# Convolution stem, forward and backward, on one core: more split leaves in both gradients, the second gelu by channel halves, x sums of batch 1 made in its input gradient, and a new order

## The chip, the cores and the metric

The kernel runs on one core of a Trainium2 chip. Its engines are TensorE (PE; PEld is its weight load), VectorE (DVE), ScalarE (ACT), GpSimd (POOL) and SyncE (SP), which in this kernel only issues DMAs. The metric is the device time of one launch in microseconds.

## The reference

```python
# x: 2 x 16000 x 256, w: 31 x 256 x 256, grad_out: 2 x 7985 x 256, bf16
def _fwd_reference(x, w, gn_gamma, gn_beta):
    h = sum over i of einsum('blc,cd->bld', x[:, i:i + 2 * L:2, :], w[i])   # L = 7985
    mu = h summed over l / L;  var = (h - mu) ** 2 summed over l / L
    h = (h - mu) / sqrt(var + 1e-5) * gn_gamma + gn_beta
    return gelu(h, approximate=True)
out, vjp = jax.vjp(_fwd_reference, x, w, gn_gamma, gn_beta)
return out, *vjp(grad_out)        # out, dx, dw, dgamma, dbeta
```

(The loop over the 31 taps is written here as one sum.) So there are three large products: the strided convolution itself, its gradient for x, and its gradient for w. Between the first and the other two lies the gelu with its normalization over the 7985 positions, forward and backward.

## The kernel before

Each of the three large products is made with fewer multiplications by splitting: taps and positions are grouped, and out of products of sums and differences the wanted ones are put together again. There are three **branches**, named A, B_ and C_, and inside a branch three **leaves** of the same names. Where a leaf is itself split once more ("split leaves" below), PE has fewer or shorter matmuls, and DVE and ACT have more sums and copies.

**Stages.** The forward product runs first, batch 0 and then batch 1, 0 to 408 us. Batch 0's gelu and its backward are done beside batch 1's forward product. Then come the input gradient (G0 for batch 0, G1 for batch 1, 408 to 801) and the weight gradient (W, 801 to the end). Batch 1's gelu (`gelu_short`) has no forward product beside it: it runs in G0, DVE lines 920 and 923 and ACT lines 916, 926 and 943. It ends with sums over all positions (`elem_finalize`, line 978 on); only when these are there can batch 1's gradient planes be made (`e_comp`, lines 1015 and 1017), spread (line 1033), subtracted (`g_sums`, line 1082) and multiplied in G1.

**Input gradient.** A batch has four chunks c, each with two halves pr and three branches. For a unit (c, pr, br), PE writes into PSUM tiles (line 1136). In a unit that the set `GOC` names ("both"), one product `pt` is shared: ACT copies its half (`g_delta`, line 1165), DVE subtracts it from the other tile (`g_seed`, line 1199), and at the end ACT keeps the results in `HO` (line 585), onto which DVE adds `GSB` (line 1213). In another unit the seed is a copy by ACT (line 585, from PSUM to PSUM), and the evacuation is an addition of 1024 on DVE (line 1217). Before, `GOC` names all of batch 1, chunk 3 of batch 0, and the branch B_ of its chunks 0 to 2.

**Leaves for W.** What W needs as stationary operands are the leaves of the gradient, transposed. `dl_turn` makes them, nine per chunk, 72 in all: two DMA transposes on SP's queue (line 319) fill one of the buffers `DNO`, and two stores of 128 KB on POOL's queue (line 314) bring it to DRAM (`dld`). W loads them from there.

**Weight gradient.** Nine nodes n, each with leaves; the set `NODES` says which leaves are split. x tiles are loaded from DRAM (1 MB each) and added on DVE (`w_add`, line 1316), or loaded as sums (`xsd`, `xssd`) that `x_sums` (line 754) has made in the forward stage, for batch 0 alone. `pair_x` (lines 1417, 1421), `pair_d` (1437), `leaf_d` (1520, 1525), `w_pairs` (1453) and `w_both` (1461) are the sums and copies around W's matmuls (line 1351).

**Order.** The program is first collected as a list of operations, each with the operations that it depends on. A table of numbers, `SEQUENCE`, then says in which order they are emitted, and that order is pinned on every engine. So what each queue does next is written in this table, and not decided anew. Nearly all DMAs, large loads and stores among them, are issued by SP in that order, and SP waits in order: behind an issue that waits for a semaphore, all later ones stand.

## Time and profile before

| what | value |
|---|---|
| runs | 1115.04, 1113.68, 1113.3 us; median 1113.68 us |
| span of the profiled execution | 1111.2 us |
| PE busy | 1086.2 us (98%) |
| DVE busy | 919.9 us (83%) |
| ACT busy | 578.9 us (52%) |
| granted TensorE clock | 1.00 throughout |
| DMA moved | 256.16 MB, mean 231 GB/s |

The profiled execution has only its span; the runs' median is 2.5 us more. An engine's share over the whole span is a mean over the stages, and the prediction goes through them one by one. In a row of a group, the number behind x is the count, then come the busy time, the mean ns of one instruction, the idle time ahead of it and what ended that.

### The profile page before, as it was taken

Reading aid. Unit: us, or ns where it says so; the run is one execution under the profiler, and the core shown is the slowest. Engines: PE = TensorE matmul, PEld = TensorE weight load, DVE = VectorE, ACT = ScalarE, POOL = GpSimd, SP = SyncE. Lnnn points to the kernel's source line nnn. Section 1 sums busy time; section 2 is a strip of 40 time slices with the busy share of each in tenths; the row PEclk is TensorE's granted clock in tenths of the full one; section 3 lists DMA queues with packets and bytes.
Section 4 is the critical chain, followed back from the end, with each engine's and each line's share of the span. In section 5 each row is a group of like instructions: output and inputs, shape, how many; then the busy total and the mean of one; then the engine's idle time right before and its main releaser. Section 6 shows DMA issues by size and latency. Waiting matters only on the chain.

```text
span 1111.2 us, 18967 instructions
## 1 busy us (share of the span) xinstructions
PE 1086.2 (98%) x7623; PEld 749.8 (67%) x7672; DVE 919.9 (83%) x900; ACT 578.9 (52%) x880; POOL 129.3 (12%) x233
## 2 busy tenths in 40 slices
...
GB/s 231 198 188 249 233 275 267 219 167 162 209 166 219 240 328 270 274 252 265 217 225 237 179 203 183 157 201 197 278 293 137 270 156 298 303 254 279 282 253 207
DMA packets 348806, 256.16 MB, mean 231 GB/s; under 512 B 234327, under 2 KB 315869, under 8 KB 343517
## 3 DMA queue, kind: packets, MB, share of 16 engines
...
HBM read 114.62 MB, written 84.45 MB: 179 GB/s over the span
## 4 chain that ended last, share of the span: by engine, by line
PE 89%; DVE 5%; issue 2%; DMA 1%; SPq 1%; ACT 1%; DVEq 0%
PE ps L1136 34%; PE ps L506 34%; PE ps L1351 21%; SPq L314 1%; DMA out_dram<-arena 1%; DVE arena L1437 1%; DVE ps L1461 1%; DMA arena<-in_w_dram 1%; DVE arena L1421 1%; DVE arena L1380 1%; DVE arena L1525 0%; DVE arena L581 0%; DVE arena L1417 0%; DVE arena L448 0%; DVE arena L1316 0%
## 5 line engine op out<-in xcount | busy, mean ns | idle before, releaser
L506 PE MATMUL ps<-arena 128*128 128x256 bf16 (+4 forms) x3464 | 396.6, 278 | 11.2 <-DMA arena<-in_x_dram 4.7
L1136 PE MATMUL ps<-arena 128*128 128x512 bf16 (+1 forms) x1787 | 388.1, 376 | 5.7 <-ACT ps L1165 3.6
L506 PEld LDWEIGHTS <-arena 128*128 128x128 bf16 x3464 | 338.2, 98 | 69.4 <-DMA arena<-in_x_dram 5.8
L1136 PEld LDWEIGHTS <-arena 128*128 128x128 bf16 x1824 | 178.5, 98 | 215.1 <-issue 2.9
L1351 PE MATMUL ps<-arena 128*128 128x256 bf16 (+1 forms) x2372 | 301.6, 289 | 3.4 <-DVE arena L1520 1.8
L1351 PEld LDWEIGHTS <-arena 128*128 128x128 bf16 x2384 | 233.2, 98 | 71.9 <-issue 2.3
L585 ACT ACTIVATE arena<-ps 128x1024 bf16<-128x1024 f32 (+1 forms) x121 | 122.1, 1022 | 213.0 <-PE ps L1351 77.3
L464 DVE TENSOR_TENSOR arena<-arena 128x2064 bf16<-128x2064 bf16 (+7 forms) x131 | 162.7, 1265 | 24.2 <-PE ps L506 23.0
L314 POOL DMA_DIRECT2D dld<-arena x144 | 104.6, 728 | 246.7 <-DMA arena<-arena 229.4
L1199 DVE TENSOR_TENSOR ps<-ps,arena 128x1024 f32<-128x1024 f32 x36 | 44.3, 1232 | 64.2 <-PE ps L1136 53.2
L1082 DVE TENSOR_TENSOR arena<-arena 128x1032 bf16<-128x1032 bf16 (+1 forms) x114 | 89.5, 813 | 9.5 <-POOL arena L1049 4.3
L551 ACT ACTIVATE ps<-ps 128x256 f32<-128x256 f32 x89 | 36.7, 412 | 85.6 <-PE ps L506 84.5
L1316 DVE TENSOR_TENSOR arena<-arena 128x4096 bf16<-128x4096 bf16 x30 | 68.3, 2287 | 0.5 <-DMA arena<-in_x_dram 0.3
L1165 ACT COPY ps<-ps 128x512 f32<-128x512 f32 x84 | 48.1, 575 | 33.7 <-PE ps L1136 30.0
L323 POOL MEMSET arena<- 128x104 bf16 (+11 forms) x52 | 12.0, 249 | 414.8 <-DVE arena L464 157.6
L923 DVE TENSOR_TENSOR arena<-arena 128x2048 bf16<-128x2048 bf16 (+1 forms) x48 | 57.5, 1197 | 3.0 <-ACT arena L926 1.3
L605 ACT ACTIVATE arena<-ps 128x512 bf16<-128x512 f32 (+1 forms) x64 | 37.0, 582 | 32.7 <-PE ps L506 28.2
L885 DVE TENSOR_TENSOR arena<-arena 128x2048 bf16<-128x2048 bf16 (+1 forms) x40 | 47.7, 1197 | 4.0 <-ACT arena L879 1.7
L1437 DVE TENSOR_TENSOR arena<-arena 128x2048 bf16<-128x2048 bf16 x40 | 48.5, 1220 | 2.4 <-PE ps L1351 2.4
L1461 DVE TENSOR_TENSOR ps<-ps,arena 128x1024 f32<-128x1024 f32 x24 | 29.1, 1227 | 19.5 <-PE ps L1351 19.5
L1453 ACT COPY ps<-ps 128x256 f32<-128x256 f32 x54 | 19.0, 360 | 47.8 <-PE ps L1351 46.7
L1525 DVE TENSOR_TENSOR arena<-arena 128x4608 bf16<-128x4608 bf16 x16 | 40.6, 2554 | 0.0
...
## 6 DMA issues: line engine op xcount, KB each, us to landing
...
dld<-arena POOLq DMA_DIRECT2D x144, 128.0 KB, 4.4
...
```

The source lines that it names most:

```text
L314: lambda: e.dma_start(out=out, in_=in_), dma=np_ * ns / 16e3 * 1.03, ns=ns, tp=SH[pk], slack=slack)
L464: lambda: nc.vector.tensor_tensor(out=o, in0=a, in1=b, op=ALU.add))
L506: yield nc.tensor.matmul(ps[:, dh, cs], lhsT=wt, rhs=mv, start=s0, stop=False, skip_group_check=True)
L585: lambda: nc.scalar.activation(out=out, in_=ps, func=ACT.Copy, scale=scale))
L885: add("DVE", dve(nf), [o], [a, b_], lambda: V.tensor_tensor(out=o, in0=a, in1=b_, op=op))
L923: add("DVE", dve(nf), [o], [a, b_], lambda: V.tensor_tensor(out=o, in0=a, in1=b_, op=op))
L1082: lambda: nc.vector.tensor_tensor(out=o, in0=a, in1=b, op=ALU.subtract))
L1136: yield nc.tensor.matmul(ps[:, e, 0:wide], lhsT=lt, rhs=mv, start=s0, stop=False, skip_group_check=True)
L1165: add("ACT", act(512), [o], [i], lambda: nc.scalar.copy(out=o, in_=i))
L1316: add("DVE", dve(4096), [o], [a, b], lambda: nc.vector.tensor_tensor(out=o, in0=a, in1=b, op=ALU.add))
L1351: yield nc.tensor.matmul(ps[:, s, c0:c1], lhsT=lt, rhs=mv, start=s0, stop=False, skip_group_check=True)
L1437: add("DVE", dve(2048), [o], [u, v], lambda o=o, u=u, v=v: nc.vector.tensor_tensor(out=o, in0=u, in1=v, op=ALU.subtract))
```

## The change

- `GOC` now names every unit, so that the twelve units of batch 0 with c below 3 and branch A or C_ become "both" units: 36 matmuls in place of 44, 24 evacuations of 1024 on DVE and 12 seeding copies on ACT less, and 12 shared products with 24 copies of 512 on ACT, 12 seeding subtractions, 24 keeps, 12 additions of 2048 and 6 subtractions of 2064 (`third_two`) more. The sums of w for the outer products (`w2_outer`) are all made when G begins.
- `NODES` has three more leaves, (4, C_), (5, C_) and (3, C_): each 96 matmuls of 256 columns in place of 64 of 512.
- `gelu_short` works on one half of the channels at a time: each of its loads, stores, DVE operations and its sigmoid becomes two of half the size. The tiles of its ring are half as large.
- `x_sums` is called for batch 1 too, eight times in G1, with a buffer of its own (`XB`). W loads these sums in place of raw x rows, and eight additions of 4096 fall away.
- To make room, the leaf buffers `DNO` go from four to two, and `GSD`, which had two, to one; several others move. In batch 0 `HO` is a single buffer in all chunks.
- `SEQUENCE` is new, 3585 operations where there were 3357.

The pieces of the new order that the prediction speaks of, as they stand in the program. First SP's queue in G0, near the end of batch 1's gelu. `DMA_TRANSPOSE arena<-arena 128x4x128` is one transpose of a leaf, `waits DMASW...` a wait for stores that POOL has issued, `dyd` and `hd` are the gelu's stores and loads. Before:

```order
L319 DMA_TRANSPOSE arena<-arena 128x4x128 [waits DMAHW0_49,DMASW5_49,DMASW3_49]
L319 DMA_TRANSPOSE arena<-arena 128x4x128 [waits DMAHW1_49]
L319 DMA_TRANSPOSE arena<-arena 128x4x128 [waits DMAHW2_49]
L314 DMA arena<-hd_2_66 128x2x1024 [waits DMAHW3_49,DVE_49,Activation_49]
L319 DMA_TRANSPOSE arena<-arena 128x4x128 [waits DMASW7_49,DMAHW4_49,DMASW6_49,DVE_49]
L319 DMA_TRANSPOSE arena<-arena 128x4x128 [waits DMAHW5_49,DMASW1_49,DMASW0_49]
L319 DMA_TRANSPOSE arena<-arena 128x4x128 [waits DMAHW6_49]
L314 DMA arena<-hd_2_66 128x2x1024 [waits DMAHW7_49,DVE_49,Activation_49]
L319 DMA_TRANSPOSE arena<-arena 128x4x128 [waits DMAHW0_49]
```

And after:

```order
L327 DMA_TRANSPOSE arena<-arena 128x4x128 [waits DMAHW2_49,DMAHW4_49,DMASW7_49,DMASW6_49]
L322 DMA dyd_1_73<-arena 128x1024 [waits DMAHW3_49]
L327 DMA_TRANSPOSE arena<-arena 128x4x128 [waits DMAHW5_49,DMASW1_49,DMASW0_49]
L327 DMA_TRANSPOSE arena<-arena 128x4x128
L327 DMA_TRANSPOSE arena<-arena 128x4x128 [waits DMAHW6_49]
L322 DMA out_dram<-arena 128x4096 [waits DMAHW7_49,DVE_49]
L322 DMA arena<-hd_2_66 128x1024 [waits DMAHW0_49,Activation_49]
L322 DMA arena<-dyd_3_71 128x2048 [waits DMAHW1_49,Pool_49]
L327 DMA_TRANSPOSE arena<-arena 128x4x128 [waits DMAHW2_49,DMASW3_49,DMASW2_49]
L327 DMA_TRANSPOSE arena<-arena 128x4x128 [waits DMAHW5_49,DMAHW3_49]
L327 DMA_TRANSPOSE arena<-arena 128x4x128 [waits DMAHW4_49,DMASW5_49,DMASW4_49]
```

The gelu's transfers now come in halves (128x1024 in place of 256x1x1024 and 128x2x1024). Where the waits for POOL's stores once spoke of stores that lay several leaves back, each leaf now waits for the two stores of the leaf before the last one.

Second, DVE at the end of batch 1's gelu; L978 and L991 are the reduction of its sums, L1082 and L1095 the subtractions of G, L1217 an evacuation of G0, L923 and L937 the gelu. Before:

```order
L1082 TENSOR_TENSOR arena<-arena 128x2x516
L1082 TENSOR_TENSOR arena<-arena 128x8x258 x2
L452 TENSOR_TENSOR arena<-arena 128x2048
L978 TENSOR_REDUCE small<-esum_113 128x4
L1082 TENSOR_TENSOR arena<-arena 128x2x516
L1217 TENSOR_TENSOR arena<-ps,arena 128x2x512
L980 TENSOR_TENSOR small<-stats,small 128x2
```

After (the first seed of batch 1 stands 25 rows behind the reduction there, and 54 rows behind it before):

```order
L1226 TENSOR_TENSOR arena<-arena 128x4x512
L937 TENSOR_TENSOR arena<-arena 128x4x232
L934 TENSOR_SCALAR arena<-arena 128x4x232
L937 TENSOR_TENSOR arena<-arena 128x4x232 x3
L991 TENSOR_REDUCE small<-esum_115 128x4
L993 TENSOR_TENSOR small<-stats,small 128x2
L994 TENSOR_TENSOR small<-small 128x2
L995 TENSOR_TENSOR small<-stats 128x2
L996 TENSOR_TENSOR small<-stats,small 128x2
```

The reduction moved behind the last operations of G0, and its small operations follow one on the other where G0's work lay between them.

Third, SP's queue at the passage from G1 to W; `dld` are the leaves that W loads, `in_x_dram` 128x4096 the x rows for `x_sums`, 128x8x512 a raw x tile for W. Before:

```order
L319 DMA_TRANSPOSE arena<-arena 128x4x128
L314 DMA arena<-dld_0_85 128x2304 [waits DMAHW6_49,PE_49]
L314 DMA arena<-dld_0_76 128x2560 [waits DMAHW7_49,PE_49]
L314 DMA arena<-dld_0_85 128x2560 [waits DMAHW0_49,PE_49]
L314 DMA out_dram<-arena 104x4096 [waits DMAHW1_49,DVE_49]
L314 DMA arena<-in_x_dram 128x8x512 [waits DMAHW5_49,DMAHW3_49,DMAHW2_49]
L319 DMA_TRANSPOSE arena<-arena 128x4x128 [waits DMASW4_49,DMASW3_49]
L314 DMA out_dram<-arena 128x4096 [waits DMAHW4_49]
L314 DMA arena<-in_x_dram 128x8x512 [waits PE_49]
```

After:

```order
L327 DMA_TRANSPOSE arena<-arena 128x4x128 [waits DMAHW1_49,DMAHW2_49,DMASW1_49,DMASW0_49]
L327 DMA_TRANSPOSE arena<-arena 128x4x128 [waits DMAHW3_49]
L322 DMA xssd_97<-arena 128x1024 [waits DVE_49]
L322 DMA dld_4_80<-zt_116 2x256 [waits DMAHW4_49]
L327 DMA_TRANSPOSE arena<-arena 128x4x128 [waits DMAHW5_49]
L322 DMA arena<-in_x_dram 128x8x512 [waits DMAHW6_49,PE_49]
L322 DMA arena<-in_x_dram 128x4096 [waits DMAHW7_49,DMAHW3_49]
L327 DMA_TRANSPOSE arena<-arena 128x4x128 [waits DMAHW0_49,DMAHW2_49,DMASW3_49,DMASW2_49]
L322 DMA arena<-dld_0_76 128x2304 [waits DMAHW1_49,PE_49]
L327 DMA_TRANSPOSE arena<-arena 128x4x128
L322 DMA arena<-dld_0_85 128x2304 [waits PE_49]
```

The last calls of `x_sums` with their loads and stores now stand between the last leaf transposes and the first leaves that W loads.

The diff, without the table and without lines that only carry addresses of other buffers along:

```diff
@@ -37,111 +37,119 @@
 SEQUENCE = """
...
@@ -348,19 +356,19 @@
-    HO = [sb(119232, 2, 4, 512), sb(GREG + 16704, 2, 4, 512)]
+    HO = [sb(119232, 2, 4, 512), sb(GREG + 20544, 2, 4, 512)]
     GSD = [sb(o, 512, dt=FP32) for o in (111040, 113088)]
-    DNO = {True: [sb(GREG + 28928 + 2048 * i, 2, 2, D) for i in range(4)], False: [sb(GREG + o, 2, 2, D) for o in (0, 2048, 25088, 27136)]}
+    DNO = {True: [sb(o, 2, 2, D) for o in (208960, 113088)], False: [sb(o, 2, 2, D) for o in (208960, 113088)]}
...
@@ -747,16 +755,19 @@
 
-    def x_sums(f):
-        load(XA, xblk(0)[:, f].rearrange("p (k r) c -> p k r c", k=2), 1 << 20, 4096)
-        for o, v in ((XA[:, :, 1:4:2], XA[:, :, 0:4:2]), (XA[:, :, 0], None)):
-            u = XA[:, :, 2] if v is None else v
+    XB = sb(GREG + 28736, 2, 4, 512)
+
+    def x_sums(f, b=0):
+        xa = (XA, XB)[b]
+        load(xa, xblk(b)[:, f].rearrange("p (k r) c -> p k r c", k=2), 1 << 20, 4096)
+        for o, v in ((xa[:, :, 1:4:2], xa[:, :, 0:4:2]), (xa[:, :, 0], None)):
+            u = xa[:, :, 2] if v is None else v
             add("DVE", dve(o.free_size()), [o], [o, u], lambda o=o, u=u: nc.vector.tensor_tensor(out=o, in0=o, in1=u, op=ALU.add))
-        load(xs_d[:, f, :, 0:2], XA[:, :, 0:2], 1 << 19, 2048)
-        load(xs_d[:, f, :, 2], XA[:, :, 3], 1 << 18, 1024)
-        o, u = XA[:, 0, 1:3], XA[:, 1, 1:3]
-        add("DVE", dve(1024), [o], [o, u], lambda: nc.vector.tensor_tensor(out=o, in0=o, in1=u, op=ALU.add))
-        load(xss_d[:, f], o, 1 << 18, 2048)
+        load(xs_d[b][:, f, :, 0:2], xa[:, :, 0:2], 1 << 19, 2048)
+        load(xs_d[b][:, f, :, 2], xa[:, :, 3], 1 << 18, 1024)
+        o, u = xa[:, 0, 1:3], xa[:, 1, 1:3]
+        add("DVE", dve(1024), [o], [o, u], lambda o=o, u=u: nc.vector.tensor_tensor(out=o, in0=o, in1=u, op=ALU.add))
+        load(xss_d[b][:, f], o, 1 << 18, 2048)
 
...
@@ -826,7 +837,7 @@
             return [sb(base - (n - j) * size, *shape) for j in range(n)]
-        tiles = [ring_of(k, 2, 4, HM) for k in rings]
+        tiles = [ring_of(k, *((2, 4, HM) if b == 0 else (4, HM))) for k in rings]
         gts = ring_of(ngt, 4, 2, XM)
...
@@ -848,8 +859,12 @@
                 oo = oos[n % len(oos)]
-                (gelu_unit if b == 0 else gelu_short)(b, c, e, [r[n % len(r)] for r in tiles],
-                                                      gt.rearrange("p k d f -> p d k f")[:, :, :, off:off + HM], oo)
+                go = gt.rearrange("p k d f -> p d k f")[:, :, :, off:off + HM]
+                if b == 0:
+                    gelu_unit(b, c, e, [r[n % len(r)] for r in tiles], go, oo)
+                else:
+                    for dh in range(2):
+                        gelu_short(b, c, e, dh, [r[(2 * n + dh) % len(r)] for r in tiles], go[:, dh])
                 n += 1
...
@@ -901,20 +916,19 @@
 
-    def gelu_short(b, c, e, tiles, go, oo):
+    def gelu_short(b, c, e, dh, tiles, go):
 
         full = tiles
-        h, y, s, z, go = (t[:, :, :, 0:wd] for t in (*tiles, go))
-        hv, dv = (d[b][c][:].rearrange("p (d e f) -> p d e f", d=2, e=2)[:, :, e] for d in (h_d, dy_d))
-        load(full[0].rearrange("p d k f -> p d (k f)"), hv, 524288, 2048, "ACT")
-        for dh in range(2):
-            for o, k, fn in ((y, 7, ACT.Identity), (z, 9, ACT.Square)):
-                sc, bi = st(b, k, dh), st(b, k + 1, dh)
-                add("ACT", act(4 * wd, 0.18), [o[:, dh]], [h[:, dh], sc, bi],
-                    lambda o=o, dh=dh, sc=sc, bi=bi, fn=fn: SC.activation(out=o[:, dh], in_=h[:, dh], func=fn, bias=bi, scale=sc))
-        nf = 8 * wd
+        h, y, s, z, go = (t[:, :, 0:wd] for t in (*tiles, go))
+        hv, dv = (d[b][c][:].rearrange("p (d e f) -> p d e f", d=2, e=2)[:, dh, e] for d in (h_d, dy_d))
+        load(full[0].rearrange("p k f -> p (k f)"), hv, 262144, 2048, "ACT")
+        for o, k, fn in ((y, 7, ACT.Identity), (z, 9, ACT.Square)):
+            sc, bi = st(b, k, dh), st(b, k + 1, dh)
+            add("ACT", act(4 * wd, 0.18), [o], [h, sc, bi],
+                lambda o=o, sc=sc, bi=bi, fn=fn: SC.activation(out=o, in_=h, func=fn, bias=bi, scale=sc))
+        nf = 4 * wd
 
...
@@ -933,14 +947,13 @@
         tt(s, y, go, ALU.mult)
-        load(dv, full[2].rearrange("p d k f -> p d (k f)"), 524288, 2048, "POOL")
+        load(dv, full[2].rearrange("p k f -> p (k f)"), 262144, 2048, "POOL")
         tt(y, s, h, ALU.mult)
         for i, t, jk in ((0, s, h), (1, y, y)):
-            for dh in range(2):
-                a0, v, j = esum[b][:, dh, i, u:u + 1], t[:, dh], jk[:, dh]
-                add("ACT", act(4 * wd, 0.19), [j, a0], [v],
-                    lambda j=j, v=v, a0=a0: SC.activation(out=j, in_=v, func=ACT.Copy, accum_out=a0))
+            a0 = esum[b][:, dh, i, u:u + 1]
+            add("ACT", act(nf, 0.19), [jk, a0], [t],
+                lambda jk=jk, t=t, a0=a0: SC.activation(out=jk, in_=t, func=ACT.Copy, accum_out=a0))
 
...
@@ -1060,7 +1073,7 @@
             for lf in (C_, A, B_):
-                ds = DNO[4 * b + c < 3]
+                ds = DNO[4 * b + c < 4]
                 o = ds[tbc[0] % len(ds)]
...
@@ -1183,17 +1196,17 @@
 
-    gsc = [0]
+    gsc, bnow = [0], [0]
 
     def g_delta(pt):
-        gsc[0] += 1
-        g_copy(GSD[gsc[0] % 2], pt[:, 0])
+        gsc[0] = 0
+        g_copy(GSD[gsc[0]], pt[:, 0])
 
             return
-        t = GSD[gsc[0] % 2]
+        t = GSD[gsc[0]]
         i = bass.AP(tensor=t.tensor, offset=t.offset, ap=[list(t.ap[0]), [0, 2], [1, 512]])
...
@@ -1203,7 +1216,7 @@
         both = (b, c, br) in GOC
-        ho = HO[pr if both else 0]
+        ho = HO[pr if b else 0]
         r2 = 0 if br == A else 1
...
@@ -1222,7 +1235,7 @@
     G3 = {(b, br, B_) for b in range(NB) for br in ORDER}
-    GOC = {(b, c, br) for b in range(NB) for c in range(NCK) for br in ORDER if 4 * b + c >= 3 or br == B_}
+    GOC = {(b, c, br) for b in range(NB) for c in range(NCK) for br in ORDER if (b, c, br) not in ()}
 
...
@@ -1304,7 +1318,7 @@
-    NODES = {(6, C_), (5, A), (0, A), (0, C_), (1, A), (2, A), (3, A), (4, A), (6, A), (7, A), (7, C_), (8, C_)}
+    NODES = {(6, C_), (5, A), (0, A), (0, C_), (1, A), (2, A), (3, A), (4, A), (6, A), (7, A), (7, C_), (8, C_), (4, C_), (5, C_), (3, C_)}
...
@@ -1329,8 +1343,8 @@
         else:
-            if b == 0 and B_ in (i1, i2):
-                load(t, xs_d[:, :, k3, {(C_, B_): 0, (B_, A): 2, (B_, C_): 1}[i1, i2]], 1 << 20, 1024)
+            if B_ in (i1, i2):
+                load(t, xs_d[b][:, :, k3, {(C_, B_): 0, (B_, A): 2, (B_, C_): 1}[i1, i2]], 1 << 20, 1024)
                 return t
...
@@ -1501,8 +1515,8 @@
             for b in range(NB):
-                if b == 0 and n in (6, 7):
-                    load(XSUM[b], xss_d[:, :, n - 6], 1 << 20, 1024)
+                if n in (6, 7):
+                    load(XSUM[b], xss_d[b][:, :, n - 6], 1 << 20, 1024)
                 else:
...
@@ -1626,13 +1640,12 @@
         load_w2(br)
-        if br == B_:
-            for lf in (C_, A):
-                w2_outer(lf, (B_,))
+        for lf in (C_, A):
+            w2_outer(lf, (MIR[br],))
     for i in range(2):
     e_load(0, 0)
-    ge = gelu_batch(1, GREG, *RINGS[1], *PACE[1])
+    ge = gelu_batch(1, GREG + 20544, *RINGS[1], *PACE[1])
     for b, c, pr, br, leaf in input_grad():
...
@@ -1650,9 +1663,8 @@
             dl_turn(b, c, leaf)
-        if (b, c, pr, br) == (0, 2, 1, A):
-            for lf in (C_, A):
-                w2_outer(lf, (A, C_))
+        if b == 1 and br == A:
+            x_sums(2 * c + pr, 1)
     plan.stage = "W"
```

19 lines of the change are left out of this document (10 added, 9 removed), and 218 rows, old and new, of the table SEQUENCE.

## The prediction

> **What bounds the kernel now.** I read the page's busy times and the engine shares of the chain that ended last, then the table of stretches, then groups of instructions, then what SP's queue waited for.
>
> ```profile
> span 1111.2 us, 18967 instructions
> PE 1086.2 (98%) x7623; PEld 749.8 (67%) x7672; DVE 919.9 (83%) x900; ACT 578.9 (52%) x880; POOL 129.3 (12%) x233
> ...
> PE 89%; DVE 5%; issue 2%; DMA 1%; SPq 1%; ACT 1%; DVEq 0%
> ```
>
> TensorE (PE) is busy for 1086.2 of 1111.2 us and makes 89% of the chain. So less PE work is worth its full length wherever the other engines can follow. Whether they can is read stage by stage (columns: stretch, its length, busy us and instructions of PE, PEld, DVE, ACT, POOL, the granted clock, DMA share, GB/s):
>
> ```profile
> 418.70:622.20 203.50, 201.84 (x935) 93.24 (x953) 180.81 (x210) 162.72 (x198) 65.41 (x110) 1.00 1.00 244
> 450.00:500.00 50.00, 49.08 (x229) 22.69 (x233) 46.63 (x50) 44.73 (x56) 17.53 (x28) 1.00 1.06 260
> 570.90:622.20 51.30, 51.04 (x237) 23.45 (x240) 39.49 (x58) 26.39 (x34) 17.33 (x27) 1.00 0.94 232
> 618.00:801.00 183.00, 182.10 (x840) 83.83 (x856) 101.39 (x107) 103.84 (x135) 55.59 (x95) 1.00 0.81 195
> 801.00:1111.20 310.20, 302.12 (x2376) 233.25 (x2385) 274.38 (x189) 73.11 (x107) 2.69 (x4) 1.00 0.83 249
> 1000.00:1050.00 50.00, 50.00 (x433) 42.27 (x432) 49.71 (x37) 11.27 (x19) 0.00 (x0) 1.00 0.86 276
> ```
>
> The first row is the input gradient of batch 0 (G0), from its first seeding subtraction on DVE (418.7) to the first of batch 1 (622.2). There PE is full, and DVE (89%), ACT (80%) and the DMA engines (1.00) nearly so. In batch 1's part (G1, 618 to 801) DVE and ACT are a little over half busy. The weight gradient (W, 801 on) has DVE at 88%, and around 1000 us PE and DVE are both full.
>
> **Part 1: less PE work, in G0 and in W.**
>
> ```profile
> L1136 PE MATMUL ps<-arena 128*128 128x512 bf16 (+1 forms) x1787 | 388.1, 376 | 5.7 <-ACT ps L1165 3.6
> L1136 PEld LDWEIGHTS <-arena 128*128 128x128 bf16 x1824 | 178.5, 98 | 215.1 <-issue 2.9
> L1351 PE MATMUL ps<-arena 128*128 128x256 bf16 (+1 forms) x2372 | 301.6, 289 | 3.4 <-DVE arena L1520 1.8
> L1351 PEld LDWEIGHTS <-arena 128*128 128x128 bf16 x2384 | 233.2, 98 | 71.9 <-issue 2.3
> ...
> L1351 PE MATMUL ps<-arena 128*128 128x512 bf16 x372 | 84.4, 379 | 0.6
> ...
> 519.61 10.53 PE ps L1136 x49
> ```
>
> The mean ns of one matmul overlaps its neighbours, so the price is busy time over number. Each matmul has its weight load, and 1824 loads stand against 1787 recorded matmuls: some records are missing, and the load count is the right divisor. The last row, a piece of the chain, gives 10.53/49 = 0.215 us per 512-column matmul. For W I take the 372 recorded 512-column ones at that price (80.0), which leaves 301.6 - 80.0 = 221.6 us for the other 2012, 0.110 each.
>
> Twelve units of G0 (three chunks, two branches, two halves) go from 44 to 36 matmuls, 84 of 512 columns and 12 of 256 in all: 84 x 0.215 + 12 x 0.110 = 19.4 us. Three more W leaves go from 64 matmuls of 512 columns to 96 of 256: 192 x 0.215 - 288 x 0.110 = 9.6 us. Together **-29.0 us** of PE work; weight loads stay 7672, and 98 ns of one still fits behind 110.
>
> The Trainium skill, "TensorE: Matmul & The Clock Gate", section "Back-to-back issue gap", gives sustained spacings of about 131 ns at 512 columns and 81 ns at 128. By these a 512-column matmul costs at most 50 ns more than a 256-column one, and the saving would be an estimated 276 x 0.05 = 13.8 us at most. The rows, 215 against 110 ns, do not agree with that at all, so this reading gets no chance of its own.
>
> **Part 2: what G0 pays.** The durations (mean ns of one stands after the comma):
>
> ```profile
> L1199 DVE TENSOR_TENSOR ps<-ps,arena 128x1024 f32<-128x1024 f32 x36 | 44.3, 1232 | 64.2 <-PE ps L1136 53.2 <-issue 8.9 <-ACT arena L1165 1.5
> L1082 DVE TENSOR_TENSOR arena<-arena 128x2064 bf16<-128x2064 bf16 x26 | 31.6, 1230 | 3.1 <-POOL arena L323 1.6 <-PE ps L1136 1.2
> L1217 DVE TENSOR_TENSOR arena<-ps,arena 128x1024 bf16<-128x1024 f32 x24 | 28.8, 1219 | 6.5 <-PE ps L1136 5.4 <-issue 1.0
> L1213 DVE TENSOR_TENSOR arena<-arena 128x2048 bf16<-128x2048 bf16 x20 | 24.4, 1222 | 19.2 <-ACT arena L585 19.1
> L923 DVE TENSOR_TENSOR arena<-arena 128x2048 bf16<-128x2048 bf16 x36 | 44.0, 1223 | 1.8 <-ACT arena L916 0.4 <-ACT arena L926 0.3
> L452 DVE TENSOR_TENSOR arena<-arena 128x1024 bf16<-128x1024 bf16 x20 | 13.4, 684 | 0.0
> L1165 ACT COPY arena<-ps 128x512 f32<-128x512 f32 x36 | 20.8, 587 | 8.6 <-PE ps L1136 8.3
> L1165 ACT COPY ps<-ps 128x512 f32<-128x512 f32 x84 | 48.1, 575 | 33.7 <-PE ps L1136 30.0 <-remote 2.6 <-DVE arena L1217 0.4
> L585 ACT ACTIVATE arena<-ps 128x1024 bf16<-128x1024 f32 x86 | 86.8, 1021 | 77.7 <-PE ps L1136 53.7 <-PE ps L506 14.8 <-remote 7.9
> L585 ACT ACTIVATE ps<-ps 128x1024 f32<-128x1024 f32 x18 | 18.1, 1006 | 5.3 <-PE ps L1136 3.3 <-remote 1.6 <-PE ps L506 0.4
> L926 ACT ACTIVATE arena<-arena 128x2048 bf16<-128x2048 bf16 x12 | 22.9, 1909 | 0.9 <-DVE arena L923 0.8
> L943 ACT ACTIVATE arena<-arena 128x1024 bf16<-128x1024 bf16 x24 | 25.1, 1047 | 2.1 <-DVE arena L923 2.0
> ```
>
> DVE gains 12 seeds (14.8), 6 subtractions of 2064 (7.4) and 12 additions of 2048 (14.7), and loses 24 evacuations of 1024 (-29.3): +7.6. A gelu operation of 2048 becomes two of half the width, 2 x 0.684 against 1.223, +0.145 each; 64 such operations, the shorter ones and the scalar ones taken at the same surplus, give +9.3. ACT gains 24 copies (12 x 0.587 + 12 x 0.575 = 13.9) and 24 keeps (24.5), loses 12 keeps inside PSUM (-12.1), and pays 16 split sigmoids (2 x 1.047 - 1.909 = 0.185 each, 3.0): +29.3. So ACT has about 192 us of work in a part that PE could now do in 184. From 162.7/203.5 = 80% ACT would have to go to 100%, and every keep and copy waits for a matmul.
>
> The order moves one thing more:
>
> ```profile
> 570.90 0.18 DVE L978 TENSOR_REDUCE small<-esum 128x4 f32<-128x32 f32 x1
> ...
> 622.20 1.23 DVE L1199 TENSOR_TENSOR ps<-ps,arena 128x1024 f32<-128x1024 f32 x1 [1.48 <-PE ps L1136]
> ```
>
> The reduction that ends batch 1's gelu sums stood 54 rows ahead of batch 1's first seed on DVE, with 39.5 us of DVE work between. It now stands 25 rows ahead, some 15 us by these durations. So less preparation of G1 lies in the part, and DVE's rows up to that seed, priced alike, come to 179 us where they were 176; but the chain of reduction, small operations, first products, sums and first matmuls of G1 has little other work left to hide behind. Bounds for the part: 184 (all of the 19.4 gained) and above 203.5 (nothing gained, and G1 starts late). The 50 us from 450 show the fullest that ACT has been over such a length, 44.73/50 = 89%; 192/0.97 = 198 is my value, nearer to the old length: 5.5 of the 19.4 are kept, a loss of **+13.9**.
>
> **Part 3: sums of x rows in G1.** Each of eight calls adds one load of 1 MB, 1 MB of stores, an addition of 2048 and two of 1024 on DVE: 8 x (1.22 + 2 x 0.684) = 20.7 us. DVE's 101 of 183 us hide that. The 16.8 MB are harder: W moved 249 GB/s at share 0.83, so 300 at full share, which makes 56 us of share, while G1 has 183 x 0.19 = 35 free. G0 shows that PE can stay full at share 1.00, so the bounds are 0 and 56 - 35 = 21. No reader waits for these sums in G1, so I take +4, nearer to nothing. At the passage to W two of these calls now share SP's queue with the first leaves that W loads: bounds 0 and one more set of transfers, some 7 us; I take +2.
>
> **Part 4: W.**
>
> ```profile
> L1316 DVE TENSOR_TENSOR arena<-arena 128x4096 bf16<-128x4096 bf16 x30 | 68.3, 2287 | 0.5 <-DMA arena<-in_x_dram 0.3
> L1437 DVE TENSOR_TENSOR arena<-arena 128x2048 bf16<-128x2048 bf16 x40 | 48.5, 1220 | 2.4 <-PE ps L1351 2.4
> L1461 DVE TENSOR_TENSOR ps<-ps,arena 128x1024 f32<-128x1024 f32 x24 | 29.1, 1227 | 19.5 <-PE ps L1351 19.5
> ```
>
> Eight additions of 4096 go (-18.3). The new split leaves add six of L1437 (7.3), two of 2048 and two of 4096 for the x pairs (2.4 + 4.6), and six of L1461 (7.4): +3.4. DVE then has 277.8 us in 300.6, 92%; the row from 1000 shows PE full beside a full DVE, so I let 1.1 of the 9.6 be lost (bounds 0 and 9.6).
>
> **Part 5: two transposed-leaf buffers instead of four.** A leaf (72 of them, all in G) is turned by two transposes on SP's queue, and stored by two DMAs on POOL's; only when these have landed is its buffer free.
>
> ```profile
> SPq L319 <- DMA dld<-arena: 41.3, 16, 7.2
> ...
> SPq L319 <- DMA dld<-arena: 36.9, 13, 7.2
> ...
> L319 SPq DMA_TRANSPOSE arena<-arena x177: 1188/1270/7553, 232.9 to 1096.4; - x177
> ...
> L314 POOL DMA_DIRECT2D dld<-arena x144: 723/723/943, 423.2 to 824.8; - x144
> ...
> dld<-arena POOLq DMA_DIRECT2D x144, 128.0 KB, 4.4
> ...
> DMA to landing us min/median/max: 2.2/4.4/8.3
> ...
> dld<-arena POOLq DMA_DIRECT2D x68, 128.0 KB, 4.7
> ```
>
> The first row is of the whole span, the second of 618 to 801: with four buffers SP already stood 36.9 us there for one to come free, and PE did not feel it. With two, pairs of leaves pass in 36 turns, and G lasts 393 us less what is gained: a turn T may take 391/36 = 10.9 us before the queue falls behind. T is the issue of a transpose (1.27), its landing (no row; taken as that of the store), the issue of a store (0.72) and its landing: 1.27 + 4.4 + 0.72 + 4.4 = 10.8 at the medians, 11.4 with the 4.7 of G1; 6.3 at the least and 18.6 at the most. Behind a waiting transpose stand, on SP's queue, the loads of dy and h, the out stores and now the x rows. I take 10.8, the medians over all: +0, with no room left.
>
> The Trainium skill, "DMA: Bandwidth & Descriptors", section "Anatomy of one DMA — SWDGE (gpsimd) path", puts such a store at about 2.0 us fixed and its bytes over 436 GB/s: an estimate of 2.3 for 128 KB. By it T would be 6.6 and the smaller ring could not slow anything. The trace agrees at its least value, 2.2, and not at its median of 4.4, which counts here.
>
> **The sum.** -29.0 + 13.9 + 4 + 2 + 1.1 + 0 = -8.0, a span of 1103.2. The runs' median, 1113.68, lies 2.5 above the profiled span, so **1106 us**.
>
> **The rivals.**
> *All of it shows.* ACT's and DVE's extra work goes into their idle time and, where that is too short (192 in 184 us on ACT), past G0's end: 1113.7 - 29.0 = 1085. For it: PE stayed full at DVE 93% (450 to 500). Against: ACT would have no pause at all.
> *Slower: the two-buffer ring.* If T is 11.5, as G1's landing times and its fuller DMA suggest, 36 x (11.5 - 10.9) = 22 us of SP standing still come out as late dy and h, idle DVE and idle PE: 1106 + 22 = 1128. Every 0.1 us of T costs 3.6; it turns to slower than before from T = 11.2. Against: a standing queue leaves the DMA engines emptier, so that landing times fall toward the least.
> *No change.* The G0 part stays at 203.5 because ACT and the chain into G1 take all that PE gave, and W's 8.5 is used up by 4 + 2 and a ring a little too slow: 1113. This is also where the split does not do, in time, what it says.
>
> **How the numbers follow.** Likeliest, part of the gain: 0.43 (1106; alone 1096 to 1111). All of it: 0.09 (1085). No change: 0.12 (1113). Slower by the ring: 0.36 (1128). What a measurement can tell from no change is about 0.2%, 1111.5 to 1115.9; so faster 0.52, same 0.12, slower 0.36. The range, 1086 to 1132, leaves out about half of the second case and the ring's cases from T = 11.6 on.
>
> **What would show it.** Right: PE's busy time near 1057; the first seed of G1 some 5 us earlier than at 622.2; ACT over 90% in G0; W's stage near 302; SP's wait for dld under twice the 41.3 us that it was for the whole span. Wrong toward slower: SP waits for dld of 100 us and more, with PE of G1 waiting for sums or hd. Wrong toward faster: the G0 part at 190 or less. If W's stage does not shrink, the DVE term was too small.

## The result, and the profile after

| | before | changed |
|---|---|---|
| median of the runs | 1113.72 us (1113.30 to 1115.04, 4 runs) | 1225.29 us (1219.63 to 1227.13, 4 runs) |
| span of the profiled execution | 1111.2 us | 1225.4 us |
| forward, to the first matmul of G | 408.0 us | 440.6 us |
| G | 393.3 us | 460.5 us |
| W | 309.9 us | 324.3 us |

The ratio is 1.0993, with a 95% interval of 1.0968 to 1.1018: slower by 10%. The prediction was 1106 us, and its range ended at 1132.

The page of the changed kernel, its header, busy times and the chain that ended last:

```profile
span 1225.4 us, 19266 instructions
PE 1091.1 (89%) x7631; PEld 755.8 (62%) x7672; DVE 961.2 (78%) x1002; ACT 604.3 (49%) x932; POOL 125.1 (10%) x233
...
DMA 30%; PE 26%; DVE 16%; SPq 12%; ACT 8%; issue 5%; POOL 1%; POOLq 0%; DVEq 0%; ACTq 0%
```

PE had 89% of the chain before and has 26% now. Transfers and SP's queue together went from 2% to 42%. So PE, although it has fewer and shorter matmuls, no longer sets the end alone. PE's busy time even rose, from 1086.2 to 1091.1 us. The stretches of the changed kernel (columns as in the prediction), first by stage, then around the passage to W:

```profile
0.00:440.50 440.50, 403.74 (x3463) 339.86 (x3464) 362.21 (x380) 233.48 (x427) 7.98 (x27) 0.98 0.83 206
440.60:675.60 235.00, 202.23 (x875) 88.16 (x892) 195.27 (x287) 195.67 (x269) 61.71 (x109) 0.97 0.83 221
675.60:901.10 225.50, 187.60 (x822) 83.68 (x838) 120.67 (x134) 101.29 (x132) 51.35 (x93) 0.95 0.83 213
901.10:1225.40 324.30, 297.45 (x2476) 244.02 (x2480) 282.98 (x202) 73.80 (x106) 4.05 (x6) 0.97 0.82 240
...
875.00:900.00 25.00, 13.97 (x57) 5.95 (x56) 11.04 (x8) 5.08 (x8) 3.15 (x5) 0.80 0.89 209
900.00:925.00 25.00, 17.44 (x132) 13.93 (x131) 16.77 (x17) 5.94 (x10) 1.74 (x3) 0.80 0.83 280
925.00:950.00 25.00, 20.05 (x174) 17.03 (x172) 19.31 (x15) 2.96 (x3) 1.44 (x2) 0.96 1.15 286
```

Every stage has become longer, the forward stage by 32.6 us although none of its operations was changed. The granted clock (third number from the end), 1.00 before, is now 0.95 to 0.98 in every stage, and 0.80 where PE stands a lot. In the three stretches from 875 to 950 PE is idle for 23.5 of 75 us; in the 75 us around the same passage before (775 to 850) it was 2.0.

The waits, by what released them: SP's queue and PE over the span, SP's queue in G1 (675 to 901), and the stores of leaves on POOL (min/median/max ns, first and last start; then KB and median us to landing):

```profile
SPq L327 <- DMA dld<-arena: 105.6, 41, 9.9
...
PE ps L1149 <- DVE ps L1212: 34.5, 14, 10.8
...
SPq L327 <- DMA dld<-arena: 76.8, 25, 9.9
...
L322 POOL DMA_DIRECT2D dld<-arena x144: 723/723/836, 446.3 to 951.8; - x144
...
dld<-arena POOLq DMA_DIRECT2D x144, 128.0 KB, 4.2
```

SP waits 105.6 us for leaf buffers where it was 41.3. The 144 stores of leaves took from 423.2 to 824.8 us before, 401.6 us or 11.2 per pair of leaves; now from 446.3 to 951.8, 505.5 us or 14.0 per pair. The last leaf is stored some 50 us into W, which needs it.

How a late transfer reaches PE can be read at PE's longest pause, 881.5 to 892.3 us: SP's issues, then DVE, then PE (start, us, what; in brackets the idle time before it and its releaser).

```profile
870.52 6.32 SPq L327 DMA_TRANSPOSE arena<-arena  x2
...
880.27 1.28 SPq L322 DMA_DIRECT2D arena<-in_x_dram  x2
...
888.83 2.29 DVE L1330 TENSOR_TENSOR arena<-arena 128x4096 bf16<-128x4096 bf16 x1 [8.55 <-DMA arena<-in_x_dram]
891.03 1.23 DVE L1212 TENSOR_TENSOR ps<-ps,arena 128x1024 f32<-128x1024 f32 x1
...
892.32 3.15 PE L1149 MATMUL ps<-arena 128*128 128x256 bf16 x8 [10.81 <-DVE ps L1212]
```

The x tile for W's addition on DVE (line 1330) was issued behind three leaf transposes. In DVE's order the addition stands ahead of a seed of G1 (line 1212), so DVE stood 8.55 us for the tile, and PE 10.81 us for the seed.

### The profile page after: what moved, and what is told of

It is laid out like the page before. It is cut to its first block, busy times and chain, and to the rows that moved or that the text cites. A ratio compares the mean times of both kernels' runs of the same rounds, so it can differ in the third digit from the quotient of the medians.

```text
span 1225.4 us, 19266 instructions
## 1 busy us (share of the span) xinstructions
PE 1091.1 (89%) x7631; PEld 755.8 (62%) x7672; DVE 961.2 (78%) x1002; ACT 604.3 (49%) x932; POOL 125.1 (10%) x233
## 4 chain that ended last, share of the span: by engine, by line
DMA 30%; PE 26%; DVE 16%; SPq 12%; ACT 8%; issue 5%; POOL 1%; POOLq 0%; DVEq 0%; ACTq 0%
PE ps L1365 14%; PE ps L514 10%; SPq L327 9%; DMA arena<-arena 9%; DMA dld<-arena 8%; DMA arena<-in_x_dram 4%; DVE arena L472 4%; SPq L322 3%; PE ps L1149 2%; DMA arena<-hd 2%; DMA out_dram<-arena 2%; DMA xsd<-arena 1%; DVE arena L1095 1%; POOL dld L322 1%; DVE arena L900 1%
## 5 line engine op out<-in xcount | busy, mean ns | idle before, releaser
L593 ACT ACTIVATE arena<-ps 128x1024 bf16<-128x1024 f32 (+1 forms) x145 | 145.9, 1020 | 220.9 <-PE ps L1365 103.9
L472 DVE TENSOR_TENSOR arena<-arena 128x2064 bf16<-128x2064 bf16 (+6 forms) x131 | 162.9, 1265 | 26.4 <-DMA arena<-in_x_dram 17.4
L1095 DVE TENSOR_TENSOR arena<-arena 128x1032 bf16<-128x1032 bf16 (+1 forms) x120 | 97.3, 834 | 10.4 <-POOL arena L331 6.6
L1212 DVE TENSOR_TENSOR ps<-ps,arena 128x1024 f32<-128x1024 f32 x48 | 58.9, 1228 | 32.6 <-ACT arena L1178 15.2
L937 DVE TENSOR_TENSOR arena<-arena 128x1024 bf16<-128x1024 bf16 (+1 forms) x96 | 64.9, 676 | 13.4 <-ACT arena L930 4.3
L1330 DVE TENSOR_TENSOR arena<-arena 128x4096 bf16<-128x4096 bf16 x22 | 50.3, 2287 | 20.3 <-DMA arena<-in_x_dram 16.9
L765 DVE TENSOR_TENSOR arena<-arena 128x2048 bf16<-128x2048 bf16 (+1 forms) x32 | 30.6, 956 | 36.6 <-DMA arena<-in_x_dram 30.3
L1451 DVE TENSOR_TENSOR arena<-arena 128x2048 bf16<-128x2048 bf16 x46 | 55.0, 1218 | 2.4 <-DMA out_dram<-arena 2.3
L331 POOL MEMSET arena<- 128x25 bf16 (+11 forms) x52 | 11.3, 247 | 399.8 <-DMA vl<-arena 140.2
L900 DVE TENSOR_TENSOR arena<-arena 128x2048 bf16<-128x2048 bf16 (+1 forms) x40 | 47.6, 1197 | 3.9 <-ACT arena L892 2.2
L1226 DVE TENSOR_TENSOR arena<-arena 128x2048 bf16<-128x2048 bf16 x32 | 39.0, 1220 | 13.0 <-ACT arena L593 12.7
L977 ACT ACTIVATE arena<-arena,stats 128x1024 bf16<-128x1024 bf16 x16 | 19.3, 1236 | 52.9 <-DMA arena<-hd 52.9
```

The lines of the kernel that those rows point to most:

```text
L472: lambda: nc.vector.tensor_tensor(out=o, in0=a, in1=b, op=ALU.add))
L593: lambda: nc.scalar.activation(out=out, in_=ps, func=ACT.Copy, scale=scale))
L900: add("DVE", dve(nf), [o], [a, b_], lambda: V.tensor_tensor(out=o, in0=a, in1=b_, op=op))
L937: add("DVE", dve(nf), [o], [a, b_], lambda: V.tensor_tensor(out=o, in0=a, in1=b_, op=op))
L1095: lambda: nc.vector.tensor_tensor(out=o, in0=a, in1=b, op=ALU.subtract))
L1212: lambda: nc.vector.tensor_tensor(out=pt[:], in0=px[:], in1=i, op=ALU.subtract))
```

## The experiments

All but the last two were run once, beside one or more runs of the kernel before with a median of 1113.7 to 1115.1 us. The times given for them are spans of the profiled execution; for the last two they are medians of the runs. Where only the order is edited, the edit is one of the table of numbers and is told in words. In the first four, line numbers are 7 higher than in the kernels that they start from; in r10, r13 and r14 one higher.

**The forward stage alone (r1).** Edit: the changed kernel, with the table's part for the forward stage put back to the old order.

> The changed kernel, in which only the operations of the forward stage (none of which the change edits) stand again in the order that they had before; gradients as in the change. Order theory: the forward stage ends at about 408 us as before in place of 440.5, G (460.7 us) and W (324.1) stay, span about 1193. Theory that the stage is slow for another reason (places in memory, the clock): it still ends near 440 and the span stays near 1225.

Measured: 1192.6 us, 32.8 less. The forward stage of r1, and of the kernel before (columns as in the prediction):

```profile
0.00:415.70 415.70, 397.31 (x3465) 338.13 (x3466) 360.72 (x380) 230.64 (x425) 7.83 (x27) 1.00 0.89 219
...
0.00:408.00 408.00, 396.63 (x3464) 338.16 (x3464) 355.62 (x375) 230.94 (x430) 8.40 (x28) 1.00 0.90 221
```

G starts at 415.7 in place of 440.6, and lasts 457 us, nearly as long as in the changed kernel (460.5). So the places of unchanged operations are worth 32.8 us of the 114.2: 24.9 in the forward stage itself, 3.5 in G and 4.4 in W. The stage does not come back to 408, as was expected; 7.7 us stay. They arise at its end: from 360 us on, where the first rows of G already stand among the forward rows on DVE, PE of r1 waits 6.3 us for DVE. One of the places can be seen at the start, on DVE. Of the changed kernel:

```profile
13.96 1.21 DVE L456 TENSOR_TENSOR arena<-arena 128x2048 bf16<-128x2048 bf16 x1
23.58 1.25 DVE L472 TENSOR_TENSOR arena<-arena 128x2080 bf16<-128x2080 bf16 x1 [8.41 <-DMA arena<-in_x_dram]
```

And of the kernel before:

```profile
12.10 2.99 DVE L464 TENSOR_TENSOR arena<-arena 128x1040 bf16<-128x1040 bf16 x3
15.01 7.02 DVE L448 TENSOR_TENSOR arena<-arena 128x2048 bf16<-128x2048 bf16 x6
```

The subtraction of 2080, which before ran without a pause (the first row names the first of its three subtractions), now stands 8.41 us for transposes of x. In SP's queue and DVE's rows, before and changed:

```
before   DVE  8 L464 TENSOR_TENSOR arena<-arena 128x8x260 [waits Pool_49]
before   SP  17 L319 DMA_TRANSPOSE arena<-in_x_dram 128x4x272 [waits DMAHW4_49,DVE_49]
changed  DVE  9 L472 TENSOR_TENSOR arena<-arena 128x8x260 [waits DMAHW4_49,DMAHW3_49,Pool_49]
changed  SP  16 L327 DMA_TRANSPOSE arena<-in_x_dram 128x4x272 [waits DMAHW3_49]
```

Before, the transpose waited for DVE; now DVE waits for the transpose. The two touch interleaved pieces of one stretch of SBUF, and the program's own list of dependencies has no edge between them: which of them waits follows from which is emitted first. This was tested by itself at the end (r17).

**The whole old order (r2), and the new order on the old operations (r3).** Edits: r2, the changed kernel's operations, those that exist in both in the old order, the others fitted in; r3, the kernel before in the new order.

> All operations of the change, but every one that the kernel before has too stands where it stood before, measured in PE work done; the added ones are fitted in at their place relative to PE. Order theory: the forward stage 408, G and W within some 20 us of before, span 1100 to 1140. Added-work theory (DVE and ACT in G0, two leaf buffers): G stays above 430 us, since the work and the buffers are those of the change: span 1150 or more.

> The kernel before with none of the edits, its operations put in the order of the change wherever the change has the same operation. Order theory: the forward stage ends at 440 (its operations and their order are then those of the change), G and W are tens of us longer than 393 and 310: span 1180 or more. Added-work theory: within some 10 us of 1111.

Measured: 1564.0 and 1378.6 us, far above both kernels. A table made for one set of operations fits another set badly: in r2 the halves of the gelu pulled other operations up to 42 us earlier, and SP waited 155.0 us for one line of ACT. Both lie far outside what either theory expected, and neither says what a part of the change costs. One reading stands, and it was expected: r3's forward stage, with the old operations in the new order, ends at 440 us (its first matmul of G is at 446), as in the changed kernel.

**Fewer leaf buffers in the kernel before (r4, r5, r7, r12).** Edit:

```diff
-                ds = DNO[4 * b + c < 3]
+                ds = DNO[4 * b + c < 3][:2]      # [:3] in r5 and r12
```

The kernel before cannot run in its own order with fewer buffers, since a leaf's transposes would stand ahead of the stores that free their buffer. So each kernel also has a changed order: r4 has the stores earlier in POOL's order; r7 and r5 have the transposes later on SP, right behind the stores that they wait for; r12 has them spaced, each pair of stores 4.3 us of PE work behind its second transpose, and the buffer's next transpose 6.5 us behind the stores.

> The kernel before with two leaf buffers in place of four, all else as it was (operations that would otherwise ask for a leaf buffer ahead of its release stand a little earlier). Ring theory of the prediction: 36 turns of T, G longer by 36 x (T - 10.9), so 1115 at T = 11.0 and 1150 at T = 12. Order theory: under 10 us of loss, since SP's standing was not what PE waited for; SP's wait for dld then goes well above 41.3 without PE noticing.

> The kernel before with two leaf buffers, as in the earlier run with two, but with the waiting transposes put later on SP's queue in place of the stores put earlier on POOL's. Ring theory: 36 turns of T = 12.5 make 450 us for G whatever stands where, so G near 450 to 480 and span 1170 to 1215. Theory that the 100 us lost there came from POOL's queue standing with small copies behind it: span under 1140.

> The kernel before with three leaf buffers in place of four; transposes that then have no free buffer yet stand a little later in the order. Ring theory: 72 leaves pass in 24 turns of three, at the T of about 12.7 us seen in the changed kernel 305 us, well inside the 393 of G: at most 10 us lost where leaves come in bursts, span 1111 to 1121. Theory that any touched order costs as much as two buffers did: near 1200.

> The kernel before with three leaf buffers, as in the run with three that took 1205 us, but spaced: a leaf's stores stand 4.3 us of PE work behind its second transpose, and the transpose that takes a buffer again 6.5 us behind the stores. Theory that it is the places in the order, set against landing times, and not the number three: SP's wait for dld falls from 162 to under 80 us and the span to 1115 to 1150. Theory that three are too few: near 1200 again.

Measured: 1212.7 (two buffers, r4), 1230.6 (two, r7), 1205.2 (three, r5), 1122.2 (three, spaced, r12). What SP waited for stores of leaves, and G or its main part (columns as before), of r5:

```profile
SPq L319 <- DMA dld<-arena: 162.0, 36, 8.7
...
408.70:855.60 446.90, 403.48 (x1787) 181.38 (x1824) 285.75 (x334) 274.17 (x345) 114.47 (x199) 0.97 0.72 193
```

And of r12:

```profile
SPq L319 <- DMA dld<-arena: 54.2, 25, 5.8
...
408.00:809.60 401.60, 392.15 (x1823) 178.88 (x1824) 289.57 (x337) 274.43 (x345) 120.09 (x201) 1.00 0.87 220
```

Two buffers, together with the order that each needs, cost the kernel before 101.5 us or 119.4 (r7 more than was expected for 36 turns), so the ring can be a cause of this size. But r5 and r12 have the same three buffers, and 83 us lie between them; for r5 the mean rate had allowed 10 us, and it lost 94. So most of that price is not the number of buffers but their places: where SP meets a transpose whose buffer is still being stored, and what stands behind it. Nor is it paid in G alone: behind the rows shown, W takes 349.6 us in r5 and 312.6 in r12 (309.9 before), and in r5 DVE stands there once 25.3 us for a leaf. The row of r5 also shows the waits' second price: PE's busy time for the same matmuls is 11.3 us longer at a clock of 0.97.

**No x sums in G1 (r9), and then four buffers in G1 (r8).** Edits, on r1; r8 has the same and the buffers:

```diff
-            if B_ in (i1, i2):
+            if b == 0 and B_ in (i1, i2):
...
-        if b == 1 and br == A:
-            x_sums(2 * c + pr, 1)
...                                                   (r8 alone)
-    DNO = {..., False: [sb(o, 2, 2, D) for o in (208960, 113088)]}
+    DNO = {..., False: [sb(o, 2, 2, D) for o in (208960, 113088, GREG + 28736, GREG + 30784)]}
```

> The changed kernel with the forward stage in its old order (1192.6 us) and without the sums of batch 1's x rows: W loads raw rows and adds them as before. Two leaf buffers stay. Ring theory: G keeps its 457 us, because 36 turns of 12.7 set it, and W pays 18 us more on DVE: span 1185 to 1205. Theory that the 16 MB of transfers in G1 slow the queue: G shorter by 20 us or more, span at most 1175.

> As the run without the sums of batch 1's x rows, and the place of their buffer is given to two more leaf buffers in G1 (four there, two in G0 as in the change). Ring theory: G1's 36 leaves no longer wait, G1 shrinks from some 225 us to about 190 and the passage to W by 20, so 50 to 60 us less than the run without the sums; SP's wait for dld halves. If the ring is not what sets G1, the two runs agree within 10 us.

Measured: r9 1207.6, r8 1202.7 us, both longer than r1's 1192.6 in all, because W, in an order into which the raw loads had to be fitted, took 353.8 and 368.8 us (319.9 in r1). The totals meet neither theory: r9 has the shorter G of the second and a span over both, and r8 is 4.9 us shorter than r9 where the ring theory said 50 to 60. G1 from its first seed, in r9 and in r8:

```profile
653.20:853.80 200.60, 182.78 (x820) 82.75 (x836) 106.69 (x118) 101.24 (x131) 52.40 (x93) 0.97 0.69 180
...
649.40:833.90 184.50, 178.79 (x822) 81.82 (x838) 106.80 (x118) 100.99 (x131) 53.82 (x93) 1.00 0.80 197
```

G as a whole takes 457 us in r1, 437 in r9, 418 in r8. So, with the ring of two, the sums of x cost G 20 us, and the small ring in G1 another 19. In r8 SP's wait for leaves in G1 is 0.9 us, and G1 lasts 184.5 us, near the 179.1 of before. What either is worth in all stays open, since W's gain from the sums could not be measured apart from its order.

**The ring's waits taken out (r10).** Edit, on r1: the stores of leaves take a constant piece of weights, so that no transpose has to wait for a store and no store for a transpose; W's operands, and so dw, are then other data.

```diff
+    WZ = sb(0, 2, 2, D)
...
-                    load(dl_d[b][...], o[:, j], 131072, 512,
+                    load(dl_d[b][...], WZ[:, j], 131072, 512,
```

> The changed kernel with the forward stage in its old order (1192.6 us); the leaves are transposed as before into two buffers, but the stores to dld take other data (a piece of the weights), so that no transpose waits for a store and no store for a transpose. The gradient for w is left out by that. The work of every engine stays. Theory that SP's standing for leaf buffers sets the gradients: G0 (221 us from first seed to first seed of batch 1) near 205, G1 (223) near 205 with the x sums still in it, the passage to W without its 20 us: span 1120 to 1145. Theory that ACT and DVE set G0: G0 stays above 215; then span 1150 or more.

Measured: 1149.2 us, 43.4 less than r1, and 4 over the range of the ring theory. Since the stores too are set free, this is what the whole tie between transposes and stores costs, POOL's waits and W's late leaves with it. G goes from 457 to 415.6 us, W from 319.9 to 316.6, the mean clock from 0.976 to 0.991. Its three parts (G0 and G1 from their first seeds, then W):

```profile
430.80:640.80 210.00, 191.82 (x863) 84.47 (x863) 186.33 (x272) 186.54 (x251) 62.42 (x106) 0.99 0.90 225
...
640.80:832.60 191.80, 182.21 (x840) 82.28 (x838) 122.22 (x137) 101.10 (x131) 49.89 (x91) 0.99 1.02 261
832.60:1149.20 316.60, 295.42 (x2481) 242.86 (x2479) 281.29 (x200) 73.70 (x106) 0.54 (x1) 0.99 0.83 240
```

With the old forward order and no ring the kernel is still 38.0 us over the 1111.2 of before: 12.1 up to the first seed (430.8, before 418.7), of which 9.0 lie in the forward stage (it ends at 417.0) and 3.1 at the start of G, 6.5 in G0 (210.0, before 203.5), 12.7 in G1 (191.8, before 179.1), 6.7 in W (316.6, before 309.9). G1's DMA share is 1.02, where it was 0.81: the sums' transfers are the one work that the change adds there (its order and the single `GSD` are new too). The sums have a reader in G1, their own additions on DVE, and these stand in DVE's order ahead of seeds. DVE of r10 in G1:

```profile
DVE arena L765 <- DMA arena<-in_x_dram: 17.0, 4, 4.7
```

**Which engine holds G0 and W (r13, r14).** Edits, on r10: r13 lets the gelu's accumulations on ACT do one quarter of their columns and `pair_d` in W do half; r14 lets the gelu's operations on DVE do one quarter.

```diff
r13
-  lambda jk=jk, t=t, a0=a0: SC.activation(out=jk, in_=t, func=ACT.Copy, accum_out=a0))
+  lambda jk=jk, t=t, a0=a0: SC.activation(out=jk[:, 0:1], in_=t[:, 0:1], func=ACT.Copy, accum_out=a0))
-            o = both(p[0][1][:, j], p[1][1][:, j], [[D, 4], [1, D]])
+            o = both(p[0][1][:, j], p[1][1][:, j], [[D, 2], [1, D]])
r14
-  lambda: V.tensor_tensor(out=o, in0=a, in1=b_, op=op))
+  lambda: V.tensor_tensor(out=o[:, 0:1], in0=a[:, 0:1], in1=b_[:, 0:1], op=op))
```

> As the run in which the stores take other data (1149.2 us, G0 210 us, W 316.6 us), with the 32 summing operations of batch 1's gelu on ACT over a quarter of their columns (some 23 us less on ACT in G0) and the pair_d subtractions of W on DVE over half of theirs (some 24 us less on DVE in W). Left out: three quarters of those sums, half of those differences. ACT theory of G0: 200 us or less there; if DVE or the order sets it, it stays within 4 us of 210. DVE theory of W: 306 us or less; if W's order sets it, it stays within 4 us of 316.

> As the run in which the stores take other data (1149.2 us, G0 210 us), with all of batch 1's gelu products and additions on DVE over a quarter of their columns (some 45 us less on DVE in G0; three quarters of these products are left out). DVE theory of G0: 200 us or less; ACT theory: within 4 us of 210. If both this and the run with less ACT work give a few us, the two share it through the chain between them.

Measured: 1153.8 and 1147.0 us. G0 of r13, then W of r13:

```profile
431.20:643.60 212.40, 191.30 (x847) 84.92 (x864) 185.95 (x272) 168.69 (x251) 64.96 (x107) 0.98 0.91 225
...
841.50:1153.80 312.30, 294.38 (x2475) 242.87 (x2479) 256.82 (x198) 73.58 (x106) 0.54 (x1) 0.99 0.82 242
```

G0 of r14:

```profile
430.90:637.90 207.00, 189.29 (x847) 84.26 (x864) 145.47 (x272) 186.28 (x250) 61.33 (x107) 1.00 0.90 228
```

18 us less of ACT leaves G0 at 212.4 (210.0 in r10). 41 us less of DVE brings 3.0. 24 us less of DVE in W brings 4.3, just over the 4 that W's order was allowed. So neither engine's load alone sets G0, and DVE's sets little of W. Both loads were not taken away together. In G0 of r10 PE waits most for ACT's copies (line 1179, 6.6 us), DVE's seeds (line 1213, 5.8) and ACT's keeps (line 593, 5.0), so the order in which PE, ACT and DVE wait for one another is the likeliest cause; no run isolates it.

**Parts of the change on the kernel before (r11, r6).** Edits: r11, the second gelu by halves alone, the order expanded where it stood; r6, the three more leaves in W alone, fitted into the order.

```diff
r11
-    def gelu_short(b, c, e, tiles, go, oo):
+    def gelu_short(b, c, e, dh, tiles, go):
-        nf = 8 * wd
+        nf = 4 * wd
r6
-    NODES = {(6, C_), ..., (8, C_)}
+    NODES = {(6, C_), ..., (8, C_), (4, C_), (5, C_), (3, C_)}
```

> The kernel before with batch 1's gelu by channel halves alone, each operation of the order replaced by its two halves, one behind the other; tiles of the same bytes, four leaf buffers. Added-work theory: 9 us more on DVE, 24 more issues on SP (some 12 us) in a part where DVE is at 89% and SP issues for 81% of the time: G0 longer by 5 to 15 us, span 1116 to 1126. If it costs nothing: 1110 to 1114.

> The kernel before with the three more split leaves of W alone; the added operations stand as in the change relative to their neighbours, everything up to 801 us as before. Prediction's term: W shorter by 9.6 us of PE work, against 21.7 us more on DVE which had 36 us left: 1104 to 1109. If DVE's fullness or the fitted-in places decide: W longer, 1112 to 1140.

Measured: 1113.6 and 1213.5 us. The halves cost 2.4 us, which is no more than the runs of the kernel before differ (1112.7 to 1116.0), and less than the 5 to 15 that were expected of added work. r6 loses 102 us, all in W (412 us), far over what was expected. The changed kernel has the same leaves in a W of 324 us, so the fitted-in places are the likely cause, and the run says nothing on the leaves themselves.

**Spaced stores with four buffers (r16).** Edit: the kernel before with all four buffers, with r12's spacing. If the standing queue of before was a cost, this should gain.

> The kernel before, four leaf buffers, with the leaves' transposes and stores spaced in the order as in the run with three (stores 4.3 us of PE work behind the second transpose, the next use 6.5 us behind the stores). Spacing theory: SP's wait for dld falls from 41 us to under 25, but PE stood for little of it: 1108 to 1114, at best 0.4% faster than before. If places in the order cost whenever they are touched: 1116 or more.

Measured: median 1118.18 us (1116.00 to 1120.91, 6 runs), ratio 1.0033 (1.0020 to 1.0046): 0.3% slower. What SP waited for stores of leaves:

```profile
SPq L319 <- DMA dld<-arena: 25.1, 12, 8.5
```

So 16.2 of the 41.3 us of standing went, and bought nothing; the time is that of the second theory, that moved places cost. That the rest was hidden too shows in the kernel before itself: in its G PE is idle for 5.5 of 393.3 us.

**One operation moved (r17).** Edit: the changed kernel, with one DVE subtraction emitted two places earlier, ahead of the x transposes. DVE, the changed kernel with - and r17 with +:

```
-L472 TENSOR_TENSOR arena<-arena 128x8x258
-L456 TENSOR_TENSOR arena<-arena 128x2048
-L472 TENSOR_TENSOR arena<-arena 128x8x260
+L472 TENSOR_TENSOR arena<-arena 128x8x260
+L472 TENSOR_TENSOR arena<-arena 128x8x258
```

> The changed kernel with one DVE subtraction of the first forward chunk (128x8x260) put two places earlier, so that it stands ahead of the four transposes of x in the program; in the change it stands behind them and DVE waits 8.4 us for their landing, with the differences of the weights behind it. Places theory: DVE's 8.4 us and PE's 8.4 us behind it go, the forward stage ends at about 432 in place of 440.5 and the whole falls from 1225 to 1215 to 1219. If that wait only hides another, the forward stage still ends at 437 or later.

Measured: median 1211.42 us (1201.16 to 1213.06, 4 runs), ratio to before 1.0841 (1.0781 to 1.0901); 14 us less than the changed kernel for one operation's place, where 6 to 10 were expected. The rows of all other engines stand in the same order; one transpose of x on SP now waits for DVE, as it did before. The start of DVE in r17:

```profile
13.55 2.39 DVE L472 TENSOR_TENSOR arena<-arena 128x2080 bf16<-128x2080 bf16 x2
15.85 11.80 DVE L456 TENSOR_TENSOR arena<-arena 128x2048 bf16<-128x2048 bf16 x10
```

The 8.41 us of standing are gone, and the forward stage ends at 430.0 us, 10.6 earlier. This is about a third of the 32.6 us that the stage lost; r1 gives back 24.9, so another 14 lie in other places of the new order, not taken apart. No version here beat the kernel before.

## Why the prediction was wrong

The 114.2 us between the two spans, by the runs:

| piece | us | from |
|---|---|---|
| places of the forward operations (24.9 of it in that stage) | 32.8 | changed kernel to r1 |
| transposes and stores tied by two leaf buffers | 43.4 | r1 to r10 |
| what is left: forward stage 9.0, start of G 3.1, G0 6.5, G1 12.7, W 6.7 | 38.0 | r10 to before |

**What bounds the kernel.** Right for before: PE. The step that failed is what followed from it, that PE work is worth its full length while others "can follow". The shares of DVE and ACT were weighed; the order in which each queue meets its waits was not. Two terms failed most: the forward stage, which had none, and the ring of two leaf buffers, taken at +0. The prediction had given "slower by the ring" a chance of 0.36, at 1128; the way was among its cases, the size was not.

**The forward stage was not in the sum.** This is the largest miss that had no term at all. "`SEQUENCE` is new" stood in the change, and Part 2, Part 3 and the pieces of order looked only at G and at the passage to W. The forward stage was taken as unchanged because its operations are. The stage lost 32.6 us, and its old places give back 32.8 in all (r1).

**Part 1, less PE work (-29.0).** The matmuls went as counted; the time did not come. From 1086.2 us PE should have come to 1057, and has 1091.1. The larger part of the 34 us is the clock. In the trace of the changed kernel it is either 1.00 or 0.50: eleven times, each time some 2 to 5 us after a pause of PE began, it falls to 0.50 for 3.4 to 10.2 us (two of these stretches, then the sum of all eleven):

```profile
886.70:896.90 10.20, 4.36 (x11) 1.72 (x12) 7.52 (x6) 1.61 (x2) 0.00 (x0) 0.50 0.61 182
...
948.20:951.60 3.40, 3.36 (x16) 2.41 (x17) 3.40 (x3) 0.00 (x0) 0.49 (x1) 0.50 0.42 60
...
sum 68.00, PE 44.55 PEld 21.71 DVE 50.57 ACT 16.78 POOL 8.89; mean PE 4.05 PEld 1.97 DVE 4.60 ACT 1.53 POOL 0.81
```

PE is busy for 44.55 of these 68.0 us; at half the clock an estimated 22 us of them are the clock's. (The mean of 0.970 over 1091 us would give 33, but it counts half-clock time in which PE stands.) In r10 the same count gives 19.2 us of PE at 0.50, so 10 of the 20 us by which 1077.2 lies over 1057. Some 11 us stay open in both. Part of them may be records: the trace of before has 7623 of its 7672 matmuls, and r11, which has the same matmuls with all recorded, shows 1090.4 us of PE.

The Trainium skill, "TensorE: Matmul & The Clock Gate", section "HAM oscillation — how this bites in real kernels", has the rule that PE should have no idle gap over about 3.4 us, since the clock is throttled then. The trace agrees in kind: full clock throughout in the kernel before, 0.970 with pauses of up to 10.8 us. It does not show that bound: after a pause of 2.33 us that ended at 948.2 the clock stood at 0.50 for 3.4 us, and after one of 3.28 us that ended at 820.1 it stayed at 1.00. So a wait of PE can cost more than its length, which the sum left out. The 13.8 us that the prediction estimates beside its rows are put together wrongly: in G0 matmuls fall away whole, and in W 288 take the place of 192, so a number times a difference is not the saving. Nothing else rests on them.

**Part 2, what G0 pays (+13.9).** Wrong in its cause. ACT was to go to about 192 us and hold G0 at 198. Its load was sized well (186.5 us in r10), but it does not hold G0: with 18 us less of it G0 is no shorter (r13), nor much with 41 us less of DVE (r14). Nor does the 0.97 by which 192 became 198 stand in a row; the one given has 0.89. G0 takes 226.3 us between first seeds (449.3 to 675.6), and 210.0 without the ring. The first seed of G1, expected some 5 us earlier than at 622.2, came 53 us later. That the gelu's halves cost little was right (2.4 us, r11, within the spread of the runs).

**Part 3, sums of x rows in G1 (+4, and +2 at the passage).** The mechanism was there (share of the DMA engines), the size was not. Taking them out shortens G by 20 us (r9), near the upper bound of 21; without the ring G1 is 12.7 over before (r10). The step that failed is that "no reader waits for these sums in G1". Their own additions wait for the x rows, 17.0 us in r10, and hold up what stands behind them on DVE, which PE waits for; and the transfers share SP's queue and the DMA engines with the leaves, which have readers too. How much each of these ways costs, no run separates. At the passage 23.5 us of PE are lost in 75, where it was 2.0 before, but how much of that is the sums' stays open: r9, without them, loses 10.3 in the 75 us around its passage, and r10, with them and without the ring's waits, 11.7.

**Part 4, W (+1.1 of loss).** 324.3 us in place of 302. Of this 7.7 went with the old forward order and without the ring (316.6 in r10), and 4.3 more with DVE relieved of 24 us (312.3 in r13). So the DVE term, too small or not, is at most a small part. The rest is open.

**Part 5, two leaf buffers (+0), and the rival.** The rival named the right mechanism, the place and the sign to look for: SP's waits for leaves of 100 us and more with PE of G1 waiting. SP's were 105.6. In G1 PE waits 28.0 us for DVE's seeds (line 1212), a wait that G1 of before does not have, and ACT 11.9 for loads of h. The term that was mis-sized is T. The sum took one transpose and one store, 1.27 + 4.4 + 0.72 + 4.4 = 10.8, though the part itself says that a leaf needs two of each, one behind the other. With two, the same rows give an estimate of 2 x 1.27 + 4.4 + 2 x 0.72 + 4.4 = 12.8 (the transposes' landing still has no row). In the trace a leaf's first store starts 12.7 us after that of the leaf two places earlier at the median and, from the rows above, 14.0 in the mean; this spacing also holds whatever else stood ahead of the transposes, so it is no clean T. By the rival's own formula 12.8 would have made 1106 + 36 x (12.8 - 10.9) = 1174, outside the range given. That formula is no good measure either: it asks 68 us for the ring, and r10 shows 43.4, about twice the 22 of the rival. That the landing times "fall toward the least" with a standing queue hardly held here: the median went from 4.4 to 4.2. It held where SP stood longer, 2.7 us in r4 and 3.2 in r7, and those runs were slow all the same.

What the ring costs depends further on places (r5 against r12, 83 us with the same three buffers). The prediction priced it as a mean rate, and a mean rate has no term for what stands behind a waiting issue.

**What was not tried.** The twelve units of G0 were not taken back alone, ACT and DVE were not relieved together, and the three leaves of W have no clean measurement: an edit of operations needs a new order, and in r2, r3 and r6 the fitted one came out 100 us and more longer. So how the 38.0 us divide between the change's parts and their places is open beyond what r9 and r13 to r14 show.
